# Numerators as 56x32 products, foldings moved together, stacks filled by another engine: a gated mix of two attentions on one core

## The chip, the core and the metric

The kernel runs on one core of a Trainium2 chip. TensorE (PE) multiplies matrices; VectorE (DVE), ScalarE (ACT) and GpSimd (POOL) work on the elements of tiles; SyncE (SP) issues the transfers (DMAs). The metric is the device time of one execution in microseconds. Every time that belongs to one line or one stage comes from one profiled execution of the kernel.

## The reference, cut to what matters

```python
def _A_ref(x, wqkv, w_phi, wo):                  # S = 2048, D = 448, H = 16, Dh = 28
    q, k, v = ((x @ wqkv) split into heads)
    pq = jnp.einsum("bhsd,hdf->bhsf", q, w_phi)
    pk = jnp.einsum("bhsd,hdf->bhsf", k, w_phi)
    phi_q = jnp.concatenate([softmax(pq), softmax(-pq)], axis=-1)      # 56 features a head
    phi_k = jnp.concatenate([softmax(pk), softmax(-pk)], axis=-1)
    kv  = jnp.einsum("bhsf,bhsd->bhfd", phi_k, v)
    z   = jnp.einsum("bhsf->bhf", phi_k)
    num = jnp.einsum("bhqf,bhfd->bhqd", phi_q, kv)
    den = jnp.einsum("bhqf,bhf->bhq", phi_q, z)[..., None] + 1e-6
    return (num / den, heads joined) @ wo

def _B_ref(x, wqkv, wo):
    scores = q k^T * Dh ** -0.5
    return (softmax(scores) v, heads joined) @ wo

g = sigmoid((x * gate_w).sum(-1))
return g * _A_ref(...) + (1 - g) * _B_ref(...)
```

All arrays are float32. Branch A is linear attention over 56 features a head, branch B full softmax attention; the two have weights of their own.

## The kernel before

The program is straight-line code for one core. On PE, DVE, ACT and POOL the order of the program is the order of the queue; SP's order is set by a planner when the kernel is built. Projections run in split precision: weights and inputs are kept as a high and a low part, and a product of the two is three passes without the low-by-low one.

**The front (0 to 64 us).** Inputs come in and are split. Units of `proj_qk` (twenty of them here, `n` from 4 to 19 in the loop, after `first_units`) project B's queries and keys. Each unit's result is cast by ScalarE (`ev`, L571), its low part made by VectorE (L572), and written out. Between them stand four `fold`s, which multiply A's key weights with the feature map `w_phi` (PE L387, ACT L391, DVE L392), the splits of the weights `wB1` and `wvA` (ACT L142, then DVE L143), and from `n` = 16 on `mx_unit`s. An `mx_unit` computes products for a running maximum of B's scores (PE L284, the tiles `pmb` and `pmd`), which ScalarE turns into `rl` (L287) and VectorE reduces into `part` (L289). The keys for it are read back from memory, with a subtraction on GpSimd (`kp`, L220). The call order of the front is the loop:

```python
        splits(n + 1)                      # n + 1 in (13, 15): a half of wB1
        ...
        if 16 <= n < 20:
            mx_unit()
        proj_qk(n, ev)
        if n in (16, 18):
            split_part(wvA_s, "wvA", 450, (n - 16) // 2)
            take_lows()
        if n in (13, 15, 17, 18):
            fold(wkA_s, "k", {13: 0, 15: 1, 17: 2, 18: 3}[n])
```

**The key phase (64 to 171 us).** Sixteen tiles of 128 tokens: `pk` (A's keys through the folded weights), `features1` and `features2` (maximum and minimum of each head on DVE L442, L443; two subtractions on POOL L445 and POOL or DVE L447; the exponential on ACT L449; the sums and their reciprocal on DVE L456, L457; the multiplication on POOL L458), `value_a`, and `kv_add`, which adds 16 products of 32 columns into `pkv`.

**The query phase (171 to 320 us).** The loop runs over `i`; `q = i - 16`, `y = q - 1`, `tb = y // 2`. For each tile of 128 queries: `pq` (PE L108), the same features, `turn` (transpositions `pft`, PE L520, copied to `fT` by ACT L523). Two tiles make a block `tb` of 256 queries, and on even `y` from 4 on (q = 5, 7 to 19, blocks 0 to 7) `numer` multiplies `fT` with `KV` (PE L532, tile `pn`). `normalize1` copies the result to `oUa` (ACT L398) and fetches the denominators (`dena`) by DMA; `normalize2` takes reciprocals (DVE L407, L408), writes them (`rda`) and reads them back spread over the partitions (`rsa`); `normalize3` multiplies (DVE L419); `normalize4` splits into `oTa` (ACT L427, POOL L428). From q = 11 on `out_a` multiplies with the output weights (`poa`, PE L108), `out_a2` applies the gate (ACT L547) and writes to `gad`. The exponentials of the features wait in the list `exps` until `take_exps`. `mx_unit`s run on.

**Values and scores (320 us to the end).** `value_b` projects B's values. Then come B's scores, 1024 products `st` with the exponentials between them and the products `pv`, with the remaining maxima (`pm`). Their operands lie in stacks (`qst`, `kst`) of 4x512 elements on 128 partitions, set to zero by `stack` on GpSimd (L817, L819) and filled by DMA. The last stretch normalizes and projects branch B.

The lines of `numer` as they stand:

```python
        for g in range(NG):
            for hh in range(2):
                n = 2 * g + hh
                nc.tensor.matmul(pn[g // 2][64 * hh:64 * hh + 64, g % 2 * 256:g % 2 * 256 + 256],
                                 KV[:, n, :], fT_of[tb][:, n, :], start=True, stop=True,
                                 tile_position=(0, 64 * hh))
```

Of the kernel before, what the change touches and what calls it, by code (L numbers as in the profile page):

```python
# [17 lines left out]
P = 128  # L18
# [21 lines left out]
def gated_mix_kernel(ctx, tc, xT, wqkB, wvB, wvA, wkAT, wqAT, phi, woA, woB,  # L40
# [396 lines left out]
    def features1(pp, nm, eng):  # L437

        pc = bd.tile([P, H, DH], F32, tag="pc", name=f"pc{nm}", bufs=2)
        nc.scalar.copy(pc, pp[:, :D].rearrange("p (h f) -> p h f", f=DH))  # L440
        ext = bd.tile([P, 2, H], F32, tag="ext", name=f"ext{nm}", bufs=3)
        nc.vector.tensor_reduce(ext[:, 0, :], pc, AX.X, ALU.max)  # L442
        nc.vector.tensor_reduce(ext[:, 1, :], pc, AX.X, ALU.min)  # L443
        f = bd.tile([P, H, 2, DH], F32, tag="feat", name=f"feat{nm}", bufs=4)
        nc.gpsimd.tensor_sub(f[:, :, 0, :], pc,  # L445
                             ext[:, 0, :].unsqueeze(2).to_broadcast([P, H, DH]))
        eng.tensor_sub(f[:, :, 1, :],  # L447
                             ext[:, 1, :].unsqueeze(2).to_broadcast([P, H, DH]), pc)
        exps.append(lambda: nc.scalar.activation(f, f, AF.Exp))  # L449
        return f  # L450

    def features2(f, nm):

        f2 = f.rearrange("p h s f -> p (h s) f")
        sm = bd.tile([P, 2 * H], F32, tag="fsum", name=f"fsum{nm}", bufs=3)
        nc.vector.tensor_reduce(sm, f2, AX.X, ALU.add)  # L456
        nc.vector.reciprocal(sm, sm)  # L457
        nc.gpsimd.tensor_mul(f2, f2, sm.unsqueeze(2).to_broadcast([P, 2 * H, DH]))  # L458
        return f.rearrange("p h s f -> p (h s f)")
# [7 lines left out]
    fk, va, fq, fT_of, num, oTs = {}, {}, {}, {}, {}, {}  # L467

    def kv_add(t):

        pf, pvv = fk.pop(t), va.pop(t)
        for g in range(NG):
            for j in range(4):
                h = 4 * g + j
                nc.tensor.matmul(pkv[32 * j:32 * j + 32, g * 56:(g + 1) * 56], pvv[:, h, :],
                                 pf[:, h * 56:(h + 1) * 56], start=t == 0 and g == 0,
                                 stop=t == NT - 1, tile_position=(0, 32 * j),
                                 skip_group_check=True)
# [15 lines left out]
    def kv_copy():  # L494

        kvT = ta.tile([P, D], F32, tag="ga", name="kvT", bufs=2)
        nc.scalar.copy(
            kvT.rearrange("p (g i f) -> p g i f", i=2, f=56),
            pkv[:, :224].rearrange("p (g f) -> p g f", f=56).unsqueeze(2).to_broadcast([P, NG, 2, 56]))
        return kvT  # L500

    def kv_out(kvT):

        pt = ps_s("pkvT")
        for g in range(NG):
            nc.tensor.transpose(pt[:112, g * P:(g + 1) * P], kvT[:, g * 112:(g + 1) * 112], ident)
        nc.vector.tensor_mul(KV, pt[:112].rearrange("p (n c) -> p n c", c=64),
                             mask_s.unsqueeze(1).to_broadcast([112, 8, 64]))

    def turn(u):  # L510

        tb, tl = divmod(u, 2)
        if tl == 0:
            fT_of[tb] = ta.tile([112, 8, 256], F32, tag="fT", name=f"fT{tb}", bufs=1)
        f = fq.pop(u)
        cut = (0, 4, 8) if u < NT - 2 else (0, 3, 6, 8)
        pt = [ps_s(f"pft{u}_{i}") for i in cut[:-1]]
        for a, b, p in zip(cut, cut[1:], pt):
            for n in range(a, b):
                nc.tensor.transpose(p[:112, (n - a) * P:(n - a + 1) * P],  # L520
                                    f[:, n * 112:(n + 1) * 112], ident)
        for a, b, p in zip(cut, cut[1:], pt):
            nc.scalar.copy(fT_of[tb][:, a:b, tl * P:(tl + 1) * P],  # L523
                           p[:112, :(b - a) * P].rearrange("p (n q) -> p n q", q=P))

    def numer(tb):

        pn = [ps_s(f"pn{tb}_{i}") for i in range(2)]
        for g in range(NG):
            for hh in range(2):  # L530
                n = 2 * g + hh
                nc.tensor.matmul(pn[g // 2][64 * hh:64 * hh + 64, g % 2 * 256:g % 2 * 256 + 256],  # L532
                                 KV[:, n, :], fT_of[tb][:, n, :], start=True, stop=True,
                                 tile_position=(0, 64 * hh))
        num[tb] = normalize1(ta, pn, f"a{tb}", 2)

    po_of = {}

# [58 lines left out]
    def splits(n):  # L597
# [3 lines left out]
        if n in (13, 15):  # L601
            split_part(wB[1], "wB1", 384, (n - 13) // 2)
# [43 lines left out]
    for n in range(4, NP):  # L646
# [9 lines left out]
        if n == 14:  # L656
# [3 lines left out]
            for v in vap:  # L660
                nc.gpsimd.memset(v[:, :, 28:32], 0.0)
                nc.gpsimd.memset(v[:, :, 28:29], 1.0)
        if 16 <= n < 20:
# [5 lines left out]
        if n in (13, 15, 17, 18):  # L669
            fold(wkA_s, "k", {13: 0, 15: 1, 17: 2, 18: 3}[n])  # L670
# [35 lines left out]
    for i in range(2 * NT + 11):  # L706
# [14 lines left out]
        if q == 2:  # L721
# [4 lines left out]
            KV = ta.tile([112, 8, 64], F32, name="KV")  # L726
# [25 lines left out]
        if y >= 9 and y % 2 and tb - 4 < 8:  # L752
            oTs[tb - 4] = normalize4(ta, num.pop(tb - 4), f"a{tb - 4}", 2)
        if q > 0:
# [21 lines left out]
        if q == 2:  # L776
            part_loads("woA", woA, D, "woA")
# [8 lines left out]
        if y >= 4 and y % 2 == 0 and tb - 2 < 8:  # L786
            numer(tb - 2)
# [27 lines left out]
    def stack(nm, keys):  # L815
        r = at.tile([P, 4, 512], F32R, name=nm)
        nc.gpsimd.memset(f32(r), 0.0)  # L817
        if keys:
            nc.gpsimd.memset(f32(r[0:1]), -1.0)  # L819
# [381 lines left out]
```

## Time and profile before

| | us |
|---|---|
| median of 3 runs | 1027.01 |
| lowest, highest | 1026.14, 1027.43 |
| the profiled execution | 1028.68 |
| its span | 1026.9 |

The span is the time from the first to the last recorded instruction; the execution's own time holds 1.8 us more around it. The granted TensorE clock was 1.00.

A row of an engine's timeline reads: start, duration, engine, line, operation, output and input tile with partitions x elements, count, and in brackets the idle time of the engine just before it with what ended it. A piece of the chain of work that ended last has start, duration, engine, tile and line. A row of busy time by stage has the stretch, its length, then busy time and number of instructions of PE, PEld (weight loads), DVE, ACT and POOL, the granted clock, the share of the DMA engines and GB/s. A row of waits names the waiting engine, tile and line, what it waited for, the total, the number of times and the longest.

### The profile page before, as it was taken

What the parts mean: (1) busy time and instruction counts of PE and PEld (TensorE: products, weight loads), DVE (VectorE), ACT (ScalarE), POOL (GpSimd) and SP (SyncE); (2) the same over time, 40 slices, a digit from 0 to 9 for tenths busy, and PEclk for the clock granted to TensorE, in tenths of its full rate; (3) what the DMA queues carried; (4) which work ended last, traced back from release to release, by engine and by line L of the source; (5) the groups of instructions that cost most, each with busy time, mean ns of one, the idle gap of its engine ahead of it and who ended that gap; (6) DMA issues with size and microseconds to landing.
All of it is one profiled execution on the core that took longest, in us unless ns stands there. A gap on an engine that the chain in (4) does not pass through costs nothing.

```text
span 1026.9 us, 17749 instructions
## 1 busy us (share of the span) xinstructions
PE 1018.9 (99%) x6344; PEld 561.2 (55%) x6344; DVE 671.0 (65%) x1335; ACT 819.3 (80%) x1534; POOL 243.5 (24%) x213
## 2 busy tenths in 40 slices
PE   9999999999999999999999999999999999999998
PEld 8878888878779433333333333333333333354555
DVE  5466567997650578788878788887878887710102
ACT  5455445677752899999999999999999999969672
POOL 1235546687336303111010110101201101011010
PEclk9999999999999999999999999999999999999999
DMA  8973110122245703233532133522313355414311
GB/s 295 312 232 106 42 51 1 61 77 75 89 130 127 153 22 81 66 69 70 126 77 73 44 69 79 128 57 52 88 43 74 87 133 133 128 53 130 125 39 54
DMA packets 64025, 98.88 MB, mean 96 GB/s; under 512 B 17952, under 2 KB 24720, under 8 KB 63936
## 3 DMA queue, kind: packets, MB, share of 16 engines
q1 hardware_dynamic: 63936, 97.74, 35.2%
q8 instruction: 50, 0.82, 0.3%
q14 instruction: 39, 0.32, 0.1%
HBM read 69.54 MB, written 27.78 MB: 95 GB/s over the span
## 4 chain that ended last, share of the span: by engine, by line
PE 92%; DMA 4%; DVE 3%; ACT 1%; issue 0%; SPq 0%; POOL 0%; ACTq 0%; POOLq 0%; DVEq 0%
PE st L850 29%; PE pv L977 25%; PE pm L321 9%; PE pk L126 4%; PE pva L126 4%; PE poa L108 4%; PE pob L108 3%; PE pq L108 2%; PE pqk L108 2%; DMA qkd<-ev 2%; PE pvb L126 2%; PE pmb L284 1%; PE pvb L108 1%; PE pft L520 1%; PE pn L532 1%; DMA gad<-ga 1%
## 5 line engine op out<-in xcount | busy, mean ns | idle before, releaser
L868 ACT ACTIVATE p<-st 128x512 f32<-128x512 f32 x1020 | 526.1, 611 | 29.5 <-PE st L850 27.8
L332 DVE TENSOR_REDUCE part<-pm 128x1 f32<-128x512 f32 x477 | 304.6, 685 | 132.3 <-PE pm L321 125.2
L850 PE MATMUL st<-qst,kst 128*128 128x512 f32 x1024 | 316.3, 430 | 0.5 <-ACT vb L694 0.5
L977 PE MATMUL pv<-p,vb 128*32 128x512 f32 x2048 | 272.8, 605 | 0.2 <-DVE oUb L398 0.2
L850 PEld LDWEIGHTS st<-qst,kst 128*128 128x128 f32 x1024 | 173.1, 187 | 137.8 <-issue 75.8
L321 PEld LDWEIGHTS pm<-kc,qc 28*128 28x128 f32 x848 | 40.5, 181 | 177.8 <-ACT p L868 169.4
L325 ACT ACTIVATE rl<-pm 128x512 f32<-128x512 f32 x212 | 126.8, 598 | 11.7 <-PE pm L321 0.3
L419 POOL TENSOR_TENSOR oUb<-oUb,rsb 128x512 f32<-128x512 f32 x15 | 19.3, 1287 | 469.0 <-DMA rsb<-rdb 251.5
L329 DVE CUSTOM_DVE_ANT_0 rl<-pm,rl 128x512 f32<-128x512 f32 x159 | 108.1, 680 | 0.0
L321 PE MATMUL pm<-kc,qc 28*128 28x512 f32 x848 | 107.1, 495 | 0.0
L977 PEld LDWEIGHTS pv<-p,vb 128*32 128x32 f32 x2048 | 40.3, 108 | 67.8 <-issue 63.6
L289 DVE CUSTOM_DVE_ANT_0 rl<-pmb,rl 128x512 f32<-128x512 f32 x88 | 57.0, 685 | 28.6 <-ACT rl L287 28.6
L988 DVE SCALAR_TENSOR_TENSOR acc<-pob,gate,acc 128x448 f32<-128x448 f32 x12 | 8.2, 684 | 86.1 <-PE pob L108 86.1
L108 PE MATMUL pqk<-XH,wB 128*128 128x512 f32 x192 | 58.8, 396 | 0.6 <-DVE ev L572 0.6
L287 ACT ACTIVATE rl<-pmd 128x1024 f32<-128x1024 f32 x44 | 45.2, 1028 | 9.2 <-PE pmd L284 3.5
L108 PE MATMUL poa<-woA_s,oTa 128*128 128x448 f32 x192 | 43.2, 374 | 0.0
L571 ACT CAST ev<-pqk 128x512 fp32r<-128x512 f32 x28 | 16.0, 588 | 34.0 <-PE pqk L108 27.0
L108 PEld LDWEIGHTS pqk<-XH,wB 128*128 128x128 f32 x192 | 35.5, 188 | 9.4 <-issue 1.5
L195 POOL TENSOR_TENSOR kc<-kc,kd 28x512 fp32r<-28x512 f32 x12 | 15.4, 1280 | 96.7 <-PE pm L321 54.9
L108 PEld LDWEIGHTS poa<-woA_s,oTa 128*128 128x128 f32 x192 | 35.0, 188 | 5.8 <-issue 2.8
L108 PE MATMUL pq<-wqA_s,XH 128*128 128x448 f32 x128 | 37.3, 374 | 0.8 <-DVE ev L572 0.8
L126 PE MATMUL pk<-wkA_s,XH 128*128 128x448 f32 x128 | 37.8, 377 | 0.0
(155 smaller groups left out, 1164.8 us busy)
## 6 DMA issues: line engine op xcount, KB each, us to landing
qkd<-ev SPq DMA_DIRECT2D x28, 512.0 KB
qst<-qkd SPq DMA_DIRECT2D x64, 224.0 KB
kst<-qkd SPq DMA_DIRECT2D x64, 224.0 KB
od<-oTb SPq DMA_DIRECT2D x48, 112.0 KB
rsa<-rda SPq DMA_DIRECT2D x8, 512.0 KB
rsb<-rdb SPq DMA_DIRECT2D x15, 256.0 KB
kc<-qkd SPq DMA_DIRECT2D x64, 56.0 KB
gad<-ga SPq DMA_DIRECT2D x16, 224.0 KB
```

What stands on the lines that cost most here:

```text
L108: nc.tensor.matmul(dst, l, r, start=i == 0, stop=i == len(todo) - 1)
L126: nc.tensor.matmul(dst[:, :n], l, r, start=i == 0, stop=i == len(todo) - 1, skip_group_check=True)
L287: nc.scalar.activation(rl, pd, AF.Relu)
L289: nc.vector.tensor_tensor_reduce(rl[:, i, :], pb[:, i, :], rl[:, i, :], 1.0, LOWEST, ALU.add, ALU.max, part[:, col + i:col + i + 1])
L321: nc.tensor.matmul(pm[j], mxs[("qc", gq)][js, qt * P:(qt + 1) * P], mxs[("kc", g, kb)][js, :], start=True, stop=True, tile_position=(32 * ...
L325: nc.scalar.activation(rl, pm[kb], AF.Relu if kb < 3 else AF.Copy)
L329: nc.vector.tensor_tensor_reduce(r, pm[j], r, 1.0, LOWEST, ALU.add, ALU.max, part[:, col + j:col + j + 1])
L332: nc.vector.tensor_reduce(part[:, col + j:col + j + 1], pm[j], AX.X, ALU.max)
L419: (nc.gpsimd if n == 1 else nc.vector).tensor_mul(oU, oU, rs)
L850: nc.tensor.matmul(st, kst_of[(g, kt // 4)][:, j, (kt % 4) * P:(kt % 4 + 1) * P], qst_of[gq][:, j, :], start=True, stop=True)
L868: nc.scalar.activation(p, st, AF.Exp, scale=SCALE)
L977: nc.tensor.matmul(pv[32 * j:32 * j + 32, :], vb[kt // 8][:, kt % 8, 4 * g + j, :], pt[j], start=kt == 0, stop=kt == NT - 1, tile_position ...
```

## The change

There are four parts.

- `numer` issues 16 products of 56 rows by 32 columns (row half `r`, column tile `c`) instead of 8 of 112 by 64, each row half into a PSUM tile of its own. For this each head's features are padded from 56 to 64 columns: four fixed tiles with zeros in the padding, filled once by GpSimd, instead of buffers of a pool. `KV` becomes a plain copy of the transposed `kvT` (which is padded too) instead of a product with a mask. Transpositions take 128 columns. The weights `woA` are loaded in the order of heads that results, in 16 transfers instead of 2. The call of `numer` moves ahead of `take_exps`, so the copies of its result stand ahead of an exponential on ScalarE. The order of PE's queue stays.
- The four foldings of A's key weights come after units 12, 13, 14 and 15, ahead of the first maxima, instead of after units 13, 15, 17 and 18.
- The halves of `wB1` are split with units 14 and 15 instead of 13 and 15.
- The zeros of the stacks `qst0`, `kst0` and `kst1` are written by VectorE instead of GpSimd.

On PE's queue the numerators have two new waits: the first product of the second row half waits for the end of the projection product ahead of the set, and the first transposition behind the set waits for the third of its four groups.

```diff
@@ -441,22 +441,24 @@
         ext = bd.tile([P, 2, H], F32, tag="ext", name=f"ext{nm}", bufs=3)
         nc.vector.tensor_reduce(ext[:, 0, :], pc, AX.X, ALU.max)
         nc.vector.tensor_reduce(ext[:, 1, :], pc, AX.X, ALU.min)
-        f = bd.tile([P, H, 2, DH], F32, tag="feat", name=f"feat{nm}", bufs=4)
-        nc.gpsimd.tensor_sub(f[:, :, 0, :], pc,
+        f = feats[feats_used[0] % 4]
+        feats_used[0] += 1
+        nc.gpsimd.tensor_sub(f[:, :, :DH], pc,
                              ext[:, 0, :].unsqueeze(2).to_broadcast([P, H, DH]))
-        eng.tensor_sub(f[:, :, 1, :],
-                             ext[:, 1, :].unsqueeze(2).to_broadcast([P, H, DH]), pc)
-        exps.append(lambda: nc.scalar.activation(f, f, AF.Exp))
+        eng.tensor_sub(f[:, :, DH:2 * DH],
+                       ext[:, 1, :].unsqueeze(2).to_broadcast([P, H, DH]), pc)
+        fx = f[:, :, :2 * DH]
+        exps.append(lambda: nc.scalar.activation(fx, fx, AF.Exp))
         return f
 
     def features2(f, nm):
 
-        f2 = f.rearrange("p h s f -> p (h s) f")
-        sm = bd.tile([P, 2 * H], F32, tag="fsum", name=f"fsum{nm}", bufs=3)
+        f2 = f[:, :, :2 * DH].rearrange("p h (s f) -> p h s f", f=DH)
+        sm = bd.tile([P, H, 2], F32, tag="fsum", name=f"fsum{nm}", bufs=3)
         nc.vector.tensor_reduce(sm, f2, AX.X, ALU.add)
         nc.vector.reciprocal(sm, sm)
-        nc.gpsimd.tensor_mul(f2, f2, sm.unsqueeze(2).to_broadcast([P, 2 * H, DH]))
-        return f.rearrange("p h s f -> p (h s f)")
+        nc.gpsimd.tensor_mul(f2, f2, sm.unsqueeze(3).to_broadcast([P, H, 2, DH]))
+        return f.rearrange("p h f -> p (h f)")
 
     exps = []
 
@@ -465,6 +467,7 @@
             exps.pop(0)()
 
     fk, va, fq, fT_of, num, oTs = {}, {}, {}, {}, {}, {}
+    feats_used = [0]
 
     def kv_add(t):
 
@@ -473,7 +476,7 @@
             for j in range(4):
                 h = 4 * g + j
                 nc.tensor.matmul(pkv[32 * j:32 * j + 32, g * 56:(g + 1) * 56], pvv[:, h, :],
-                                 pf[:, h * 56:(h + 1) * 56], start=t == 0 and g == 0,
+                                 pf[:, h * 64:h * 64 + 56], start=t == 0 and g == 0,
                                  stop=t == NT - 1, tile_position=(0, 32 * j),
                                  skip_group_check=True)
 
@@ -493,9 +496,11 @@
 
     def kv_copy():
 
-        kvT = ta.tile([P, D], F32, tag="ga", name="kvT", bufs=2)
+        kvT = ta.tile([P, 2, 512], F32, tag="rs", name="kvT", bufs=2)[:, 0, :]
+        k4 = kvT.rearrange("p (g i f) -> p g i f", i=2, f=64)
+        nc.gpsimd.memset(k4[:, :, :, 56:], 0.0)
         nc.scalar.copy(
-            kvT.rearrange("p (g i f) -> p g i f", i=2, f=56),
+            k4[:, :, :, :56],
             pkv[:, :224].rearrange("p (g f) -> p g f", f=56).unsqueeze(2).to_broadcast([P, NG, 2, 56]))
         return kvT
 
@@ -503,38 +508,50 @@
 
         pt = ps_s("pkvT")
         for g in range(NG):
-            nc.tensor.transpose(pt[:112, g * P:(g + 1) * P], kvT[:, g * 112:(g + 1) * 112], ident)
-        nc.vector.tensor_mul(KV, pt[:112].rearrange("p (n c) -> p n c", c=64),
-                             mask_s.unsqueeze(1).to_broadcast([112, 8, 64]))
+            nc.tensor.transpose(pt[:, g * P:(g + 1) * P], kvT[:, g * P:(g + 1) * P], ident)
+        nc.vector.tensor_copy(KV, pt)
 
     def turn(u):
 
         tb, tl = divmod(u, 2)
         if tl == 0:
-            fT_of[tb] = ta.tile([112, 8, 256], F32, tag="fT", name=f"fT{tb}", bufs=1)
+            fT_of[tb] = ta.tile([P, 8, 256], F32, tag="fT", name=f"fT{tb}", bufs=1)
         f = fq.pop(u)
         cut = (0, 4, 8) if u < NT - 2 else (0, 3, 6, 8)
         pt = [ps_s(f"pft{u}_{i}") for i in cut[:-1]]
         for a, b, p in zip(cut, cut[1:], pt):
             for n in range(a, b):
-                nc.tensor.transpose(p[:112, (n - a) * P:(n - a + 1) * P],
-                                    f[:, n * 112:(n + 1) * 112], ident)
+                nc.tensor.transpose(p[:, (n - a) * P:(n - a + 1) * P],
+                                    f[:, n * P:(n + 1) * P], ident)
         for a, b, p in zip(cut, cut[1:], pt):
             nc.scalar.copy(fT_of[tb][:, a:b, tl * P:(tl + 1) * P],
-                           p[:112, :(b - a) * P].rearrange("p (n q) -> p n q", q=P))
+                           p[:, :(b - a) * P].rearrange("p (n q) -> p n q", q=P))
 
     def numer(tb):
 
         pn = [ps_s(f"pn{tb}_{i}") for i in range(2)]
-        for g in range(NG):
-            for hh in range(2):
-                n = 2 * g + hh
-                nc.tensor.matmul(pn[g // 2][64 * hh:64 * hh + 64, g % 2 * 256:g % 2 * 256 + 256],
-                                 KV[:, n, :], fT_of[tb][:, n, :], start=True, stop=True,
-                                 tile_position=(0, 64 * hh))
+        for gp in range(2):
+            for r in range(2):
+                for c in range(4):
+                    n, rows = 4 * gp + c, slice(64 * r, 64 * r + 56)
+                    h = 2 * n + r
+                    nc.tensor.matmul(pn[r][32 * c:32 * c + 32, gp * 256:gp * 256 + 256],
+                                     KV[rows, 32 * h:32 * h + 32], fT_of[tb][rows, n, :],
+                                     start=True, stop=True, tile_position=(64 * r, 32 * c),
+                                     skip_group_check=True)
         num[tb] = normalize1(ta, pn, f"a{tb}", 2)
 
     po_of = {}
+
+    def load_woA(b):
+
+        raw = stg.tile([P, 2, 512], F32, tag="stg", name=f"woA_raw{b}")
+        for i in range(2):
+            for c in range(4):
+                h = 8 * i + 2 * c + b // 2
+                nc.sync.dma_start(raw[32 * c:32 * c + 32, i, :D],
+                                  woA[32 * (h % 4):32 * (h % 4) + 32, h // 4, :])
+        return raw[:, :, :D]
 
     def out_a(t):
         tb, tl = divmod(t, 2)
@@ -598,8 +615,8 @@
 
         if n % 4 == 1 and n < 12:
             split_x(n // 4 + 1, raws.pop(("x", n // 4 + 1)))
-        if n in (13, 15):
-            split_part(wB[1], "wB1", 384, (n - 13) // 2)
+        if n in (14, 15):
+            split_part(wB[1], "wB1", 384, n - 14)
         take_lows()
 
     def first_units():
@@ -660,14 +677,17 @@
             for v in vap:
                 nc.gpsimd.memset(v[:, :, 28:32], 0.0)
                 nc.gpsimd.memset(v[:, :, 28:29], 1.0)
+            feats = [bd.tile([P, H, 64], F32, name=f"feat{i}") for i in range(4)]
+            for f in feats:
+                nc.gpsimd.memset(f[:, :, 56:], 0.0)
         if 16 <= n < 20:
             mx_unit()
         proj_qk(n, ev)
         if n in (16, 18):
             split_part(wvA_s, "wvA", 450, (n - 16) // 2)
             take_lows()
-        if n in (13, 15, 17, 18):
-            fold(wkA_s, "k", {13: 0, 15: 1, 17: 2, 18: 3}[n])
+        if 12 <= n < 16:
+            fold(wkA_s, "k", n - 12)
         if n == 10:
             pair_query(0, 0)
             pair_load(0, 0)
@@ -723,7 +743,7 @@
             ta_s = ExitStack()
             ta = ta_s.enter_context(tc.tile_pool(name="ta", bufs=1, reuse_waits="tile"))
             stg = ta_s.enter_context(tc.tile_pool(name="stg", bufs=2, reuse_waits="tile"))
-            KV = ta.tile([112, 8, 64], F32, name="KV")
+            KV = ta.tile([P, 512], F32, name="KV")
             kvT = kv_copy()
             ps_s_.close()
             ps = ps_s_.enter_context(tc.tile_pool(name="psq", bufs=1, space=PSUM, reuse_waits="tile"))
@@ -751,6 +771,8 @@
             mx_unit()
         if y >= 9 and y % 2 and tb - 4 < 8:
             oTs[tb - 4] = normalize4(ta, num.pop(tb - 4), f"a{tb - 4}", 2)
+        if y >= 4 and y % 2 == 0 and tb - 2 < 8:
+            numer(tb - 2)
         if q > 0:
             take_exps(int(q < NT))
         if q == 3:
@@ -774,7 +796,7 @@
         if q == 1:
             ev_s.close()
         if q == 2:
-            part_loads("woA", woA, D, "woA")
+            raws["woA"] = [load_woA(b) for b in (0, 2)]
         if q == 11:
             part_loads("wvB", wvB, D, "wvB")
         if q in (4, 6):
@@ -783,8 +805,6 @@
             split_part(wvB_s, "wvB", D, (q - 14) // 3)
         if q == 1:
             gates()
-        if y >= 4 and y % 2 == 0 and tb - 2 < 8:
-            numer(tb - 2)
         if y < 9 or y % 2:
             if y >= 2 and y - 2 < NT:
                 turn(y - 2)
@@ -814,9 +834,10 @@
 
     def stack(nm, keys):
         r = at.tile([P, 4, 512], F32R, name=nm)
-        nc.gpsimd.memset(f32(r), 0.0)
+        eng = nc.vector if nm in ("qst0", "kst0", "kst1") else nc.gpsimd
+        eng.memset(f32(r), 0.0)
         if keys:
-            nc.gpsimd.memset(f32(r[0:1]), -1.0)
+            eng.memset(f32(r[0:1]), -1.0)
         return r
 
     def load_stack(r, src, c, parts):
```

## The prediction

> **What bounds the kernel now.** I read the page first: busy time of each engine, then the chain of work that ended last.
>
> ```profile
> PE 1018.9 (99%) x6344; PEld 561.2 (55%) x6344; DVE 671.0 (65%) x1335; ACT 819.3 (80%) x1534; POOL 243.5 (24%) x213
> ...
> PE 92%; DMA 4%; DVE 3%; ACT 1%; issue 0%; SPq 0%; POOL 0%; ACTq 0%; POOLq 0%; DVEq 0%
> ```
>
> TensorE is busy for 1018.9 us, 99% of the span: the kernel is TensorE's list of work and little else. Taking work off that list pays only where nothing else is about as late. So the second view is busy time by stage (stretch; its length; then PE, PEld, DVE, ACT, POOL; granted clock), and the third TensorE's waits ahead of the scores.
>
> ```profile
> 64.00:171.00 107.00, 107.00 (x922) 89.77 (x924) 66.28 (x140) 52.31 (x89) 57.85 (x50) 1.00 0.22 69
> ...
> 198.00:214.00 16.00, 15.77 (x99) 12.61 (x97) 15.45 (x27) 12.40 (x22) 13.09 (x8) 1.00 0.27 72
> 214.00:228.00 14.00, 14.00 (x94) 10.56 (x93) 13.34 (x30) 11.47 (x18) 12.23 (x10) 1.00 0.33 85
> ...
> 242.00:256.00 14.00, 14.00 (x87) 11.36 (x86) 9.48 (x20) 10.66 (x17) 10.17 (x8) 1.00 0.22 73
> ...
> 320.00:337.00 17.00, 17.00 (x84) 15.40 (x83) 0.00 (x0) 4.16 (x9) 16.77 (x10) 1.00 0.81 172
> ```
>
> ```profile
> PE pmd L284 <- DVE part L289: 1.0, 3, 0.5
> ```
>
> The stages differ. From 64 to 171 us TensorE has no gap, so time won ahead of it is kept. From 198 to 228 VectorE is nearly as full as TensorE (15.45 of 16, 13.34 of 14), and GpSimd close behind (13.09, 12.23): a shorter TensorE list leaves those two as the bound. From 242 VectorE has room. TensorE's waits for the key maxima (pmd) are three, 1.0 us together; each lies at one of the places below.
>
> **Foldings and the wB1 split.** First rows of ACT, PE and DVE in the front, then pieces of the chain.
>
> ```profile
> 39.84 0.83 ACT L142 CAST wB<-wB_raw 128x768 fp32r<-128x768 f32 x1 [3.33 <-DMA wB_raw<-in_wqkB_dram]
> ```
>
> ```profile
> 42.32 0.73 PE L108 MATMUL pqk<-XH,wB 128*128 128x512 f32 x2 [0.56 <-DVE ev L572]
> ```
>
> ```profile
> 62.24 0.62 DVE L392 TENSOR_TENSOR wkA_s<-pwk,wkA_s 128x448 fp32r<-128x448 f32 x1
> 62.77 0.68 DVE L289 CUSTOM_DVE_ANT_0 rl<-pmb,rl 128x512 f32<-128x512 f32 x1
> ```
>
> ```profile
> 45.74 7.35 DMA wvA_raw<-in_wvA_dram
> ...
> 55.80 0.60 DVE rl L289
> ...
> 56.47 0.50 PE pmd L284 x2
> ...
> 59.73 0.88 PE pwk L387 x8
> ...
> 64.24 0.48 PE pmd L284 x2
> ```
>
> At 39.84 ScalarE stands 3.33 us behind the cast of wB1's first half, with evictions queued behind it; that becomes TensorE's gap of 0.56 at 42.32. The changed order puts the eviction and the first folding ahead of that cast, so the gap goes. But the gain is lost again at 56.47: that product waits for VectorE's maxima (55.80), which stand behind the split of wvA, and wvA lands 7.35 us after 45.74. SP issues it at the same place in its order as before, behind the same units, so 56.47 stays. Behind it one folding is gone (59.73, 0.88): that is the most the front can give. The fifth set of maxima, at 64.24, then waits for VectorE instead. Its own queue gets shorter by the folding's subtraction, from 62.24 to 62.77, 0.53 us; the wvA subtraction ahead of it does not move. So the product at 64.24 comes 0.53 earlier, and everything after it: **−0.53**, with 0 and −0.88 as ends. The four foldings now run one after each of four units while ScalarE and VectorE, with 3.33 us of idle time at 39.84, have room for their casts.
>
> **Numerators.** Pieces of the chain: the numerators, then products of the scores.
>
> ```profile
> 195.85 1.88 PE pn L532 x16
> ...
> 340.40 1.00 PE pv L977 x8
> 341.39 0.43 PE pm L321
> ```
>
> ```profile
> 222.28 0.37 PE L108 MATMUL pq<-wqA_s,XL 128*128 128x448 f32 x1
> 222.48 0.57 PE L108 MATMUL pq<-wqA_s,XH 128*128 128x448 f32 x2
> ```
>
> One numerator set is 8 products in two passes, 16 records, in 1.88 us. They run in pairs (two column halves), so 8 pairs of 0.235 each. The new form has 16 products of 56 rows by 32 columns, 32 records. If two row halves and four column tiles run at once, 8 go together and four batches remain: 4 x 0.235 = 0.94. That four column tiles do is shown by pv: 8 records of 512 columns in 1.00 us, two batches of 0.50, where one product of such a length takes 0.43. That row tiles do is shown by the pieces of maxima, whose products of 28 rows at several row positions share 0.43.
>
> Two waits are new on TensorE's queue: the second bank's first product waits for the last projection product to end, and the first transposition after the set waits for its third group. Everything of TensorE stands behind each. What such an end costs: a projection product is recorded for 0.37 from 222.28, and the next starts 0.20 later, so waiting for an end exposes 0.17. The first wait I take at 0.17 in full, the second at half, 0.08, as the fourth group runs meanwhile. 0.94 + 0.17 + 0.08 is about 1.2, so 0.68 less for each of eight sets. The ends: nothing overlaps beyond today's pairs, 1.88 + 0.34 = 2.2 (0.34 dearer); the waits cost nothing, 0.94 (0.94 saved).
>
> A rule speaks against this. The Trainium skill, "TensorE: Matmul & The Clock Gate", Part 3 (Packing small matmuls), says that a weight load overlaps products in flight only when its row group differs. By it each batch's load on rows already in use would lie open, and the set would save less than I say. The trace disagrees: at pv the second batch loads the same rows, and 0.50 for a batch against 0.43 leaves 0.07 for such a load, which the 0.235 above, itself a batch with its load, holds already.
>
> Of the padded features, the transpositions take 128 columns of weights instead of 112 and stream the same 128: I take nothing, from 0 to 0.02 for each of 16 turns.
>
> **What passes through.** TensorE's shortening counts only where the next wait allows it. PE from 213 us, DVE, POOL and the chain:
>
> ```profile
> 213.73 0.50 PE L284 MATMUL pmd<-kp,qp 28*128 28x512 f32 x2 [0.23 <-DVE part L289]
> ```
>
> ```profile
> 222.40 0.08 DVE L289 DVE_READ_ACCUMULATOR2_ANT part<- 128x1 f32 x1
> ```
>
> ```profile
> 223.54 2.52 POOL L428 TENSOR_TENSOR oTa<-oUa,oTa 128x512 fp32r<-128x512 f32 x2
> ```
>
> ```profile
> 223.05 0.42 PE pmb L284
> 223.48 1.88 PE pn L532 x16
> 225.37 2.66 PE poa L108 x12
> ```
>
> Sets 0 and 1 (q = 5, 7) lie in the stretch where VectorE is full, and the product at 213.73 waits for VectorE already: their 1.36 us turn into a longer wait there, 0. Set 2 follows at once, at 214.2; the next maxima at 223.05 need VectorE's reduction that ends at 222.48, so TensorE can be early by 0.5 at most. VectorE's list in between is the same. Set 3, at 223.48, would bring the poa at 225.37 another 0.68 forward, but poa reads what GpSimd makes from 223.54 to 226.06, its second half late in the poa: again about 0.5. Together **−0.55** up to 228.
>
> ```profile
> 251.10 0.35 DVE L408 RECIPROCAL dena<-dena 128x32 f32<-128x32 f32 x1
> ...
> 265.51 0.18 DVE L407 TENSOR_SCALAR dena<-dena 128x32 f32<-128x32 f32 x1 [3.06 <-DMA dena<-oUa]
> ```
>
> ```profile
> 269.79 9.47 DMA gad<-ga
> ...
> 282.29 0.50 PE pmd L284 x2
> ```
>
> Set 4, between 228 and 242, has free engines around it and passes in full: **−0.68**. Behind it a chain of transfers takes over: the reciprocals at 251.10 are written, read back, awaited by VectorE (265.51, idle 3.06), written and read again, and the gated rows issued behind them at 269.79 land 9.47 us later; ScalarE, held by that, is late with the maxima for 282.29. Sets 5, 6 and 7 start behind that reciprocal and lie inside the chain: their 2.0 us become a longer wait at 282.29. If the transfers give way they add up to −2.0.
>
> **Exponentials behind the copies.** ACT and DVE near 215 us, where it is tightest:
>
> ```profile
> 215.25 0.94 ACT L449 ACTIVATE featq<-featq 128x896 f32<-128x896 f32 x1
> 216.09 1.06 ACT L398 COPY oUa<-pn 128x512 f32<-128x512 f32 x2
> ```
>
> ```profile
> 217.66 1.08 DVE L456 TENSOR_REDUCE fsumq<-featq 128x32 f32<-128x896 f32 x1
> ```
>
> Now the copies go first: with the set at 214.2 done by 215.4, copies to 216.5 and the exponential to 217.4, ahead of VectorE's sum at 217.66. Hidden with 0.2 us to spare; if the set still takes 1.88, it is 0.4 late. Behind these copies wait that exponential, the copies of fT and the next projection's copy, all with the same or more room.
>
> **GpSimd's multiplication, now over four axes.** POOL rows:
>
> ```profile
> 44.75 2.65 POOL L220 TENSOR_TENSOR kp<-kp,kt 28x512 fp32r<-28x512 f32 x2 [11.01 <-DMA kt<-qkd]
> ...
> 186.77 1.71 POOL L458 TENSOR_TENSOR featq<-featq,fsumq 128x896 f32<-128x896 f32 x1 [3.37 <-DVE fsumq L457]
> 188.44 0.94 POOL L445 TENSOR_TENSOR featq<-pcq,extq 128x448 f32<-128x448 f32 x1
> ...
> 201.54 2.36 POOL L458 TENSOR_TENSOR featq<-featq,fsumq 128x896 f32<-128x896 f32 x1 [0.73 <-DVE fsumq L457]
> ```
>
> The subtraction L445 already writes 28 out of 56 and takes 0.94 for 448 elements, 2.10 ns each; the multiplication 1.71 for 896, 1.91 ns. At the dearer rate it would be 1.88, +0.17 each, within its idle 0.73. I take 0, ends 0 and four times 0.17 in the tight stretch, +0.7. VectorE's sums and subtractions over the padded rows have the same element counts: 0 likewise. The four fills of the features' padding, and kvT's, go where GpSimd waits anyway, the four in its 11.01 us ahead of 44.75: 0; without that cover they would delay kp, and with it SP's wvA.
>
> **Stacks, and woA's loads.** A row of SP:
>
> ```profile
> 92.74 0.62 SPq L131 DMA_DIRECT2D woA_raw<-in_woA_dram  x1
> ```
>
> The five fills go to VectorE at 320, which is idle for 17 us while TensorE has no gap: 0 either way; without that cover the end would be where GpSimd is now. woA comes in 16 small transfers instead of 2, the second load at 92.74 with 0.62 of SP; at that each, 14 more take 8.7 us of SP. woA is first multiplied at 225.37, 130 us later, and the loads behind them on SP are for keys of later maxima: 0, or at worst 8.7 of delay to one such set.
>
> **The sum.** −0.53 − 0.55 − 0.68 = −1.8 us. The profiled execution's own time of 1028.68 becomes 1026.9; it stands 1.67 above the median of the runs, 1027.01, so the forecast is **1025.2 us**. A measurement of this kernel can tell about 0.2%, 2.05 us, from no change: faster means below 1024.96, slower above 1029.06.
>
> **The rivals.**
> (a) *Every set passes.* For it: TensorE's share of the chain, 92%. Against: the waits just shown. −0.53 − 8 x 0.68 = −6.0: 1021.0 us. Chance 0.15.
> (b) *Row halves take turns*, through the new waits or one path into the array: sets of 1.88 to 2.2, and only the front pays, less some tenths at the exponentials: 1026.5. The trace has no products of 56 rows in two halves. Chance 0.17.
> (c) *Slower: the four-axis multiplication.* If GpSimd pays for it as for a second run over the data (+1.71), each of the 8 of q = 4 to 11 goes 0.98 beyond its idle 0.73, where GpSimd is nearly full: +7.8, so 1025.2 + 7.8 = 1033. It decides from +0.73 each, and makes "slower" from about +1.2. Against: L445's rate. Chance 0.13.
> (d) *The change doesn't do what it says in the front*: the earlier first folding waits for its weights, or wvA stays last to the end: the front gives 0 or costs up to a folding, 0.88; 1025.7 to 1026.6, with somewhat more if later units go with it. Chance 0.05.
>
> **How the numbers follow.** The forecast case has 0.5. Its own spread goes by the bounds (front 0 to −0.88, VectorE's stretch 0 to −1.0, set 4 from 0 to −0.94, part of the chain's −2.0, GpSimd up to +0.7): about 1022.5 to 1027.5. With the threshold at 1024.96 that is 0.24 faster, 0.26 same. Faster: 0.24 + 0.15 = 0.39. Same: 0.26 + 0.14 of (b) + 0.03 of (d) = 0.43. Slower: 0.13 + 0.03 + 0.02 = 0.18. The range, 1021.0 to 1030.0, holds all but the worse part of (c) and the better part of (a).
>
> **What would show it.** Right: pn x32 at about 1.2 us; no wait at 42, one near 63 before pmd; pmd's waits longer near 213, 222 and 282, with 282.29 at about 281.0. Wrong: pn near 1.9; L458 above 1.9 uncontended; pmd at 282 earlier by 3 us or more, which is (a); idle VectorE in 198 to 228 waiting for GpSimd or the exponential.

## The result, and the profile after

The changed kernel takes 1025.4 us, median of 22 runs (1024.23 to 1027.3), against 1026.99 for the kernel before (22 runs): ratio 0.9985, 95% interval 0.9979 to 0.9990. That is 1.6 us faster, within the 0.2% that the prediction called the same. Its profiled execution took 1025.96 us, with a span of 1024.2. Of the page, busy time and the chain:

```profile
PE 1013.9 (99%) x6472; PEld 557.3 (54%) x6472; DVE 680.7 (66%) x1340; ACT 820.0 (80%) x1534; POOL 236.2 (23%) x213
...
PE 89%; DVE 4%; DMA 4%; ACT 1%; SPq 1%; issue 1%; POOL 0%; DVEq 0%; ACTq 0%; POOLq 0%
```

TensorE's list is 5.0 us shorter (1018.9 to 1013.9) between these two traces and 3.3 us shorter between a second pair (1017.0 and 1013.7, e8 and e6 below); the time holds 1.6 of it. The stages of the prediction, and TensorE's waits before 340 us:

```profile
198.00:214.00 16.00, 13.90 (x110) 10.73 (x110) 15.45 (x26) 11.72 (x20) 12.60 (x8) 0.97 0.31 73
214.00:228.00 14.00, 14.00 (x121) 10.40 (x120) 11.41 (x26) 10.82 (x18) 11.68 (x9) 0.79 0.30 80
...
242.00:256.00 14.00, 14.00 (x109) 11.55 (x108) 10.04 (x20) 11.06 (x18) 10.33 (x8) 1.00 0.24 74
...
320.00:337.00 17.00, 17.00 (x82) 15.03 (x81) 7.06 (x4) 5.74 (x10) 14.50 (x10) 1.00 0.88 179
```

```profile
PE pmd L284 <- DVE part L289: 3.7, 4, 2.1
```

VectorE is as full from 198 to 214 as before (15.45), and TensorE has lost 2.1 us there to one wait. What is new stands behind the busy times: the granted clock is 0.79 from 214 to 228, where it was 1.00. Pieces of the chain show what that did:

```profile
213.25 0.79 PE pmd L284 x2
214.04 1.89 PE pn L538 x32
215.93 1.90 PE pft L524 x8
217.82 3.19 PE pq L108 x11
...
222.47 2.27 PE pq L108 x11
...
225.18 1.04 PE pn L538 x32
```

A set of numerators takes 1.04 at full clock, 1.89 behind the wait; the same projection 2.27 and 3.19. By finer stretches the clock is 0.50 from 213 to 219.5; it falls just before the wait ends at 213.25. Starts of the same products, in the first trace of each kernel and in a second one (e8 and e6 below), in us:

| | before | before, e8 | changed | changed, e6 |
|---|---|---|---|---|
| first pk | 64.65 | 64.49 | 64.01 | 64.54 |
| set 3 | 223.42 | 223.26 | 225.11 | 224.25 |
| set 4 | 237.68 | 237.52 | 238.52 | 237.71 |
| set 5 | 251.90 | 251.74 | 251.94 | 251.11 |
| poa behind the pmd of 282 | 282.73 | 281.52 | 280.68 | 279.83 |
| first scores | 336.19 | 334.81 | 334.29 | 333.54 |
| span | 1026.9 | 1025.0 | 1024.2 | 1023.4 |

Two executions of one kernel differ by 1.9 us before and 0.8 after. The first trace of before was a late one, and 1.05 of its lateness lies between set 5 and the poa of 282. Second trace against second trace: nothing won up to set 4 (+0.19), then −0.82 at set 4 alone (set 5 at −0.63), −1.06 more up to the poa, +0.42 back, and −0.3 in the rest.

### The profile page after: what moved, and what is told of

Same layout as the page of the kernel before. It is cut to its first block, busy times and chain, and to the rows that moved or that the text cites. A ratio compares the mean times of both kernels' runs of the same rounds, so it can differ in the third digit from the quotient of the medians.

```text
span 1024.2 us, 18042 instructions
## 1 busy us (share of the span) xinstructions
PE 1013.9 (99%) x6472; PEld 557.3 (54%) x6472; DVE 680.7 (66%) x1340; ACT 820.0 (80%) x1534; POOL 236.2 (23%) x213
## 4 chain that ended last, share of the span: by engine, by line
PE 89%; DVE 4%; DMA 4%; ACT 1%; SPq 1%; issue 1%; POOL 0%; DVEq 0%; ACTq 0%; POOLq 0%
PE st L871 29%; PE pv L998 25%; PE pm L321 9%; PE pk L126 4%; PE pva L126 4%; PE poa L108 4%; PE pob L108 3%; PE pq L108 2%; PE pqk L108 2%; DMA qkd<-ev 2%; PE pvb L126 2%; PE pvb L108 2%; PE pmb L284 1%; PE pft L524 1%; DVE rl L289 1%; DMA wvA_raw<-in_wvA_dram 1%
## 5 line engine op out<-in xcount | busy, mean ns | idle before, releaser
L589 DVE TENSOR_TENSOR ev<-pqk,ev 128x512 fp32r<-128x512 f32 x28 | 19.0, 690 | 28.4 <-ACT ev L588 28.3
```

## The experiments

Theory A: TensorE runs into VectorE's list at 213, and the long wait brings half clock, which costs on top. Rivals: the half clock comes otherwise, or costs nothing because the transfers behind it set the end. The ratio of the changed kernel, 0.9985, is the footing.

**e1: the wait filled.** `numer` issues its 16 products twice for blocks 0 and 1:

```diff
+        for gp, r, c in order * (2 if tb < 2 else 1):
```

> The numerator sets 0 and 1 are issued twice each, with the same result; everything else is as in the changed kernel. In the changed kernel TensorE waits 2.10 us for VectorE at 213.25 and then runs at a granted clock of 0.50 for about 6 us, to 219. Theory A (the idle time lowers the clock, and the slow stretch is a loss of its own): twice 1.03 us of added products per set fill the wait, the clock stays at 1.00, set 2 starts within 0.2 us of the changed kernel's 213.97, set 3 at about 223.4 instead of 225.11, and the kernel becomes faster although it does 2.1 us more work: about -1.4 us, 1024.0. Theory B (the slow clock comes at this point whatever TensorE does, or what is won is lost again at the waits behind it): same as the changed kernel within 0.5 us, 1025.4, or slower by up to 2.1.

Measured 1028.23 against 1026.34: 1.0023 (1.0014 to 1.0031), slower. TensorE's rows, then VectorE's, then SP's of e1 and of the changed kernel:

```profile
212.68 0.50 PE L284 MATMUL pmd<-kp,qp 28*128 28x512 f32 x2 [0.45 <-DVE part L289]
...
221.43 0.79 PE L284 MATMUL pmd<-kp,qp 28*128 28x512 f32 x2 [3.54 <-DVE part L289]
```

```profile
218.59 0.18 DVE L407 TENSOR_SCALAR dena<-dena 128x32 f32<-128x32 f32 x1 [4.57 <-DMA dena<-oUa]
```

```profile
207.84 0.55 SPq L413 DMA_DIRECT2D rsa<-rda  x1
208.49 1.14 SPq L401 DMA_DIRECT2D dena<-oUa  x2
```

```profile
207.01 1.20 SPq L401 DMA_DIRECT2D dena<-oUa  x2
208.36 0.53 SPq L413 DMA_DIRECT2D rsa<-rda  x1
```

The wait at 213 is filled (0.45), and there the clock stays at 1.00. But on SP, whose order the planner sets, the small reads of the denominators now stand behind the large read-back `rsa`: they landed about 10 us after their issue, VectorE stood 4.57 us, and TensorE's wait came back as 3.54 at 221, with a clock of 0.50 from 219.5 to 226. So it was no test of the cost; it shows the price of that order on SP, and that the half clock went where the wait went.

**e2: useful work into the wait.** At q = 9 `numer` is called ahead of `mx_unit`.

```diff
+        if q == 9:
+            numer(tb - 2)
         if q in (0, 1) or q >= 8:
             mx_unit()
```

> At q = 9 alone the numerators of block 2 stand ahead of the maxima that wait for VectorE, so 1.03 us of useful products lie inside the wait of 2.10. Theory A (a wait of such a length lowers the clock): the wait is about 1.07 now; if that is short enough the clock stays at 1.00 and set 3 starts at about 222.4 to 223.4 instead of 225.11, -1.7 to -2.7 there, of which VectorE's list passes at least -1.4: 1024.0. If 1.07 us lowers the clock all the same, only the 1.0 us of set 2 is won, or nothing. Theory B (what is won here is lost at the waits behind it): 1025.4, same.

Measured 0.9982 (0.9973 to 0.9991), not to be told from the changed kernel.

```profile
213.05 0.50 PE L284 MATMUL pmd<-kp,qp 28*128 28x512 f32 x2 [1.08 <-DVE part L289]
```

```profile
211.00:214.00 3.00, 1.92 (x32) 0.95 (x17) 3.00 (x6) 1.58 (x4) 1.58 (x2) 0.99 0.69 176
214.00:217.00 3.00, 3.00 (x12) 2.78 (x11) 2.93 (x10) 2.47 (x4) 2.47 (x2) 0.50 0.29 96
217.00:220.00 3.00, 3.00 (x20) 2.35 (x20) 2.96 (x7) 1.52 (x3) 2.49 (x3) 0.94 0.23 46
```

A wait of 1.08 brought half clock too, for 3.3 us instead of 6.7; set 3 started at 222.46.

**e3 and e4: the front alone, and the change without it.** e3 is the kernel before with the new places of the foldings and of wB1's split; e4 is the changed kernel with the old ones.

```diff
-        if n in (13, 15, 17, 18):
-            fold(wkA_s, "k", {13: 0, 15: 1, 17: 2, 18: 3}[n])
+        if 12 <= n < 16:
+            fold(wkA_s, "k", n - 12)
```

> The kernel before with the foldings after units 12 to 15 and the wB1 split at units 14 and 15, nothing else. Theory A (the front's gain of 0.64 us at the start of the key phase reaches the end): -0.5 to -0.65 us against the kernel before, with the key phase starting at 64.0. Theory B (the wait chain of transfers at 251 to 282 us takes it up): pmd at 282.29 where it was, 0.0.

> The changed kernel with foldings and wB1 split as before. Theory A (front and numerators add): key phase at 64.65 again, set 2 still behind a wait of about 2 us and at half clock, and 0.6 slower than the changed kernel: -1.0 against the kernel before. Theory B (the wait at 213 comes from the two changes together): the wait at 213 is under 1.5 us and the clock stays at 1.00, so it is no slower than the changed kernel.

Measured 0.9997 (0.9989 to 1.0006) for e3, 0.9986 (0.9977 to 0.9995) for e4. Alone the front is worth nothing that can be told from zero, and without it the change is worth as much as with it. But the interval of e3 runs from −1.1 to +0.6 us, so that the whole −0.53 is passed is as open as that none is. e4 keeps the wait at 213 (2.04) and the half clock behind it, so these do not come from the front. Third and fifth pmd of the front, in e8 (before) and e6 (changed):

```profile
56.31 0.50 PE pmd L284
...
64.08 0.48 PE pmd L284 x2
```

```profile
56.88 0.50 PE pmd L284 x2
64.12 0.50 PE pmd L284 x2
```

From third to fifth it is 7.77 before and 7.24 now: −0.53, and within 0.02 of that in every trace. But the third came at 55.92 to 57.17 in the four traces with the old front and at 55.78 to 57.08 in the ten with the new: it moves more from one execution to the next than the front's whole term.

**e5: VectorE's list shortened.** The two subtractions for woA go to GpSimd, two and three iterations earlier.

```diff
-        if q in (4, 6):
-            split_part(woA_s, "woA", D, (q - 4) // 2)
+        if q in (2, 3):
+            split_part(woA_s, "woA", D, q - 2, nc.gpsimd)
```

> The changed kernel with the two subtractions that make woA's low half moved from VectorE (1.09 us at 200.76, 1.03 at 208.91) to GpSimd, and with the casts at q = 2 and 3, where GpSimd waits. VectorE's list ahead of the maxima at 213 is 2.1 us shorter. Theory A (VectorE's list sets the wait there, and a wait of 1 us or more brings the half clock): the wait of 2.10 falls under 0.5, the clock stays at 1.00 through 230, set 3 starts at 221.5 to 222.5 instead of 225.11, and the kernel gains 2 to 3.5 us over the changed one if what stands behind passes it: 1022 to 1023.5 on the same footing as 1025.4. Theory B (the half clock comes at this place whatever TensorE waits): the granted clock falls at 213 to 214 again. Theory C (the chain of transfers from 251 to 282 sets the end of this phase): set 3 early as in A, but the end unchanged, 1025.4.

```profile
201.19 1.09 PE L524 MATMUL pft<-ident,feat 128*128 128x128 f32 x8 [0.97 <-POOL feat L460]
205.83 1.16 PE L538 MATMUL pn<-fT,KV 56*32 56x256 f32 x32 [1.31 <-ACT fT L527]
```

The wait at 213 is gone, with it the half clock there, and set 3 starts at 223.31, 0.94 ahead of e6. That is short of the 221.5 to 222.5 that theory A expected. Instead TensorE waits 0.97 for GpSimd's features and 1.31 for ScalarE's copies of them (fT), and these brought no half clock in this trace. The poa behind 282 starts at 279.69 against 279.83 in e6: nearly nothing is left of the lead. A piece of the chain of e5 shows what holds it there, a transfer of gated rows:

```profile
267.49 8.74 DMA gad<-ga
```

Measured 0.9981 (0.9973 to 0.9990), beside 0.9983 (0.9974 to 0.9992) for the changed kernel on the same chip. What is won at 223 is lost again by 282, as theory C said. Eight of e5's eleven executions have a mean granted clock of 1.000, and they are no faster than the changed kernel (medians 1025.05 and 1025.04).

**e6 and e8: the two kernels once more**, for second traces.

> The changed kernel once more, for a second trace and as the footing of the others. Every theory: 1.6 us faster than before. Theory A: again a wait near 2.1 at 213, half clock behind it, set 3 within 0.3 of 225.11. The transfers: the denominators of block 5, issued behind the read-back of block 4, land 8.5 us later in the first trace; if their times vary from one execution to the next, this one differs by a microsecond.

> The kernel before once more, for a second trace. If the transfer chain of 251 to 282 us has a fixed length, the denominators of block 5 land 10.0 us after their issue again and pmd starts at 282.3; if the first trace had a slow execution of it, they land in about 8.5 us and pmd starts near 281, and what the change wins behind 251 is smaller than the two first traces say.

e6 has the wait again, half clock for about 3.4 us, and set 3 at 224.25, not within 0.3 of 225.11. Here the clock falls at about 215.6, 1.8 us after the wait has ended:

```profile
213.82 0.50 PE L284 MATMUL pmd<-kp,qp 28*128 28x512 f32 x2 [2.11 <-DVE part L289]
```

```profile
214.00:217.00 3.00, 3.00 (x43) 2.22 (x43) 2.93 (x7) 2.59 (x4) 1.71 (x2) 0.76 0.47 117
217.00:220.00 3.00, 3.00 (x11) 2.52 (x10) 2.97 (x7) 1.27 (x3) 2.48 (x3) 0.67 0.30 80
```

Of e8, SP and VectorE near 260, and all its waits for the maxima:

```profile
255.32 1.14 SPq L401 DMA_DIRECT2D dena<-oUa  x2
```

```profile
264.04 0.18 DVE L407 TENSOR_SCALAR dena<-dena 128x32 f32<-128x32 f32 x1 [1.75 <-DMA dena<-oUa]
```

```profile
PE pmd L284 <- DVE part L289: 0.4, 2, 0.2
```

The denominators of block 5 take 8.72 us here (264.04 − 255.32), 9.98 in the trace that the prediction read. TensorE does not wait there (its pmd starts at 281.09): for the kernel before, the chain held TensorE in a late execution only. With TensorE earlier it can hold it again, as the chain of e5 shows.

**e7 and e12: the old place of `numer`**, behind `take_exps`, the rest as changed; e12 is e7 once more.

```diff
+        if y >= 4 and y % 2 == 0 and tb - 2 < 8:
+            numer(tb - 2)
         if y < 9 or y % 2:
```

> The changed kernel with the call of numer where it was before, behind take_exps: on ScalarE the exponential stands ahead of the copies again. Theory A (the place is hidden by the full VectorE, as the prediction has it): same as the changed kernel within 0.3 us. Rival (the earlier copies bring denominators about 0.9 us earlier, and the transfer chain that follows is late without it): slower than the changed kernel by 0.5 to 1 us, with the wait for dena near 264 longer by as much.

> e7 once more. Theory A (numer ahead of take_exps lets TensorE run ahead into one wait of 2.1 us that brings the half clock; behind take_exps the same time is spent in three waits of under 0.7, at full clock): again no half clock at 213 to 220, and 0.5 to 1 us faster than the changed kernel, 2.4 to 2.7 faster than before. If e7 was chance: 1.6 faster than before.

Measured 0.9978 (0.9968 to 0.9988) and 0.9982 (0.9973 to 0.9992): at least as fast as the changed kernel, not shown to be faster. In e7 the wait of 2.1 falls apart into four:

```profile
198.74 0.67 PE L108 MATMUL pq<-wqA_s,XH 128*128 128x448 f32 x2 [0.68 <-ACT oUa L398]
206.90 0.67 PE L108 MATMUL pq<-wqA_s,XH 128*128 128x448 f32 x2 [0.51 <-ACT oUa L398]
213.94 0.50 PE L284 MATMUL pmd<-kp,qp 28*128 28x512 f32 x2 [0.40 <-DVE part L289]
216.91 0.67 PE L108 MATMUL pq<-wqA_s,XH 128*128 128x448 f32 x2 [0.43 <-ACT oUa L398]
```

The clock stays at 1.00 through these. e12 has the same four and, against its expectation of waits under 0.7, one more, also at full clock:

```profile
224.11 0.50 PE L284 MATMUL pmd<-kp,qp 28*128 28x512 f32 x2 [1.03 <-DVE part L289]
```

The place ahead of the exponential is not shown to save time; it gathers the idle time in one wait.

**e9: a wait without the change.** The kernel before, with the maxima and minima of q = 8 taken three times.

```diff
+        for _ in range(3 if nm == "q8" else 1):
```

> The kernel before, with its old numerators, foldings and stacks; at q = 8 VectorE takes the maximum and the minimum of the features three times instead of once (same result), 4 x 0.53 = 2.1 us more on VectorE ahead of the maxima that TensorE waits for at 213. Theory A (a wait of about 2 us is enough to bring the half clock, whatever the numerators look like): the wait of 0.23 becomes about 2.3, the granted clock falls to 0.50 at 213 to 217 for 3 us or more, and set 3 starts 1.5 us or more later than the 2.1 of the added work says: 227 or later instead of 223.4. Theory B (the half clock comes from the new small products): clock 1.00 throughout, set 3 at 225.5.

Measured 1.0035 (1.0023 to 1.0047), 3.3 us slower for 2.1 of work.

```profile
216.66 0.50 PE L284 MATMUL pmd<-kp,qp 28*128 28x512 f32 x2 [2.42 <-DVE part L289]
```

```profile
217.00:221.00 4.00, 4.00 (x32) 3.02 (x31) 3.93 (x11) 3.74 (x6) 2.86 (x3) 1.00 0.30 93
```

In this trace a wait of 2.42 brought no half clock, against theory A. The mean granted clock is known for all six executions: 1.000 in two (1028.84 and 1029.78 us), 0.998 or 0.997 in four (1029.92 to 1032.40). Where it fell in those four is not recorded, and of the 31 executions of the kernel before that ran beside them, five are at 0.998 too. So it is likely, not shown, that the added wait brings half clock in some executions. What goes with a mean of 0.998 is about 0.8 us in e9 (medians 1029.31 and 1030.06, two executions each) and 2.2 us in the kernel before (1026.75 for 25 at 1.000, 1028.96 for the five). A mean of 0.999 says little: in e7's trace the clock is low only in the last 2 us, where TensorE has no work. Of the changed kernel's 33 executions 30 were at 0.998 or below; of e7's and e12's 24, four.

**e10: e7 with half of woA on GpSimd.**

> As e7 (numer called behind take_exps), and the first half of woA split at q = 2 with its subtraction on GpSimd, which waits 2.61 us ahead of 194. VectorE's list from 201 to 213 is 1.1 us shorter. Theory A (VectorE's list sets this stretch): set 2 starts 0.8 to 1.1 us earlier than in e7, the clock stays at 1.00, and the kernel is 0.5 to 1 us faster than e7. Rival (GpSimd, or the transfers behind 251, sets it as well): same as e7.

Measured 1.0004 (0.9995 to 1.0013), 1.8 us worse than e12 beside it, which neither theory had. The subtraction did not fall into GpSimd's gap, but behind the next multiplication, and held up the features; TensorE waited for the copies, and from about 200 to 203.7 the clock was 0.50 (0.87 in the mean of the stretch):

```profile
195.71 2.32 POOL L143 TENSOR_TENSOR woA_s<-woA_raw,woA_s 128x896 fp32r<-128x896 f32 x1
```

```profile
200.44 1.11 PE L108 MATMUL pq<-wqA_s,XH 128*128 128x448 f32 x2 [2.58 <-ACT oUa L398]
```

```profile
198.00:211.00 13.00, 10.56 (x77) 8.85 (x78) 8.45 (x16) 9.37 (x16) 8.79 (x8) 0.87 0.15 39
```

**e11: the stacks on GpSimd again.**

```diff
-        eng = nc.vector if nm in ("qst0", "kst0", "kst1") else nc.gpsimd
+        eng = nc.gpsimd
```

> The changed kernel with all stacks filled by GpSimd, as before. Theory A (the fills are hidden by TensorE's work from 320 to 337): same as the changed kernel, within 0.3 us. Rival (the fill of the first stacks gates the first scores): later first scores, slower by up to 2 us.

Measured 1.0001 (0.9993 to 1.0010): the whole gain is gone, and theory A of this run with it.

```profile
334.81 0.70 PE L871 MATMUL st<-qst,kst 128*128 128x512 f32 x2 [1.06 <-DMA kst<-qkd]
```

```profile
319.80 0.53 POOL L707 MEMSET vb<- 128x512 f32 x1 [10.57 <-DMA woB_raw<-in_woB_dram]
320.39 0.33 POOL L708 MEMSET vb<- 128x128 f32 x1
320.56 1.87 POOL L838 MEMSET qst<- 128x2048 f32 x1
```

The first scores wait 1.06 us for a stack and start at 334.81, where e8 has them too, without a wait. GpSimd starts its fills at 320.56, in e8 at 318.30, because the fill of the second value tile ahead of them waits 10.57 us, until 319.80 (310.38 in e8). In the changed program that fill waits for a transfer of `woB`, which SP issues at about 318.2 in e11, behind a gate of ScalarE's; in e8 it waits for nothing, and the fill of `qst` behind it waits 6.99 us for a product. That the larger padded tiles moved it in memory is likely, and wasn't tried. VectorE's fills, 1.76 us each from 317.46 in e6, go around that queue.

**What the runs say of theory A.** The half clock follows the long wait and not the new products: it moved with the wait in e1 (to 219.5) and e10 (to 200), and the traces of e5, e7 and e12, with the same products and no wait over 1.31, have none there. What it costs at the end is not shown for the changed kernel: e5, almost free of it, is no faster, and the changed kernel's two executions at 1.000 (1025.94 and 1024.01) lie on either side of its usual time. No version was shown to beat the changed kernel, and no run has the numerators or the stacks alone on the kernel before, so what each of them is worth is read from the traces and from e11.

## Why the prediction was right, point by point

The forecast of −1.8 us met a measured −1.6, but as a sum of terms of which two were wrong in opposite ways: VectorE's stretch lost time, and sets 5 to 7 won some. That they nearly cancel is luck.

- **Numerators, 1.2 us a set.** 1.02 to 1.05: the row halves do run side by side, and the two new waits cost 0.1 together, not 0.25. A set saves 0.84. Rival (b) is gone.
- **The front, −0.53.** Right in size behind the third pmd (7.77 to 7.24). That this product stays where it was is neither shown nor refuted: its start varies by over 1 us with either front. In six of the ten traces with the new front the chain to it runs through TensorE's own list and ScalarE's casts and not through wvA's transfer; with the old front TensorE's own list sets it in one of four. Whether the −0.53 reached the end is open.
- **VectorE's stretch, −0.55.** That sets 0 and 1 turn into a longer wait at 213 was right (0.23 to 2.10). That TensorE would then be early by 0.5 at sets 2 and 3 was wrong: at set 3 it was 1.69 late in the first traces and 0.99 in the second, and at the start of set 4 still 0.84 and 0.19, where the sum has it 1.08 early. The wait brought half clock, which no part of the sum held. The Trainium skill, "TensorE: Matmul & The Clock Gate", Part 1, has the clock fall to half after a whole idle window of about 3.4 us, with windows that run freely. These traces agree with the free-running window (the clock fell before the wait's end in the first trace, 1.8 us after it in e6) and with slow stretches of one or two such lengths (3.3 and 6.7 us); they disagree on the idle time, since 2.10 and 1.08 were enough.
- **Set 4, −0.68.** −0.80 in the first traces and −0.82 in the second: it passes in full, and a set saves more than the sum says.
- **Sets 5 to 7, absorbed.** −1.06 in the second traces, −2.09 in the first. The step that failed took the chain of transfers from one execution for a bound. Of the 1.9 us by which that trace is longer than e8, 1.05 were lost in this chain, so the same lateness was in the forecast twice: as a bound, and in the correction to the median by 1.67. What TensorE meets first in the changed kernel is another wait, which the sum does not name: 0.58 at 261 in both traces, for VectorE's list with the split of `wvB` in it (2.51 us from 257.69).
- **Stacks, 0 either way.** Wrong: without VectorE's fills the change gains nothing that can be measured (e11). The prediction named TensorE's work as the cover and did not ask whether GpSimd would be free as early as before.
- **Exponentials, 0.** No cost in time is shown (e7, e12), but the place is not without effect: it made one wait of several. In the first trace VectorE did stand 0.71 for the exponential, behind a set at half clock; in e6 it did not.

```profile
217.92 1.09 DVE L458 TENSOR_REDUCE fsumq<-feat 128x32 f32<-128x896 f32 x1 [0.71 <-ACT feat L451]
```

- **GpSimd's multiplication, 0.** Right; it takes 1.70 uncontended, where it took 1.71:

```profile
205.42 1.70 POOL L460 TENSOR_TENSOR feat<-feat,fsumq 128x896 f32<-128x896 f32 x1 [0.73 <-DVE dena L407]
```

Rival (c) is gone. Rival (a) came half true: up to the poa of 282, sets 4 to 7 passed 2.9 us of their 3.4 (4 x 0.84) in the first traces, 1.9 in the second.

## What to carry to other kernels

Shortening the work of an engine that is already held by another one saves nothing there and leaves idle time. The order of the queues decides whether that is one wait (2.1 us here) or several (0.4 to 0.7 in e7), and on TensorE a wait of 1.08 us or more could bring 3.3 to 6.7 us of half clock. A wait for a transfer is read from two executions before it is taken for a bound. When tiles change size, look at what each engine's first instruction in the next phase waits for, since another tile may now lie in its place (likely here, not tried).

## What the runs showed of the hardware

- Between 60 and 340 us the traces have eleven waits of TensorE over 1 us, in a list that is otherwise nearly full. Half clock came with seven (1.08 to 3.54 us: the two of the changed kernel, e1, e2, e4, e10, e11), for about 3.4 us in five and 6.7 in two. It did not come with 1.31 (e5), 2.42 (e9), 1.03 (e12) and 1.06 (e11).
- Two reads of 8 KB issued 0.65 us behind a read-back of 512 KB landed about 10 us after their issue (e1), so the order of the two on SP decides a wait of 4.57 us.
